# A seven-product block multiplication in three PSUM banks instead of four, with a new order of work

## The chip, the cores and the metric

The kernel runs on one core of one Trainium2 chip. The core has a matrix engine (TensorE, PE in the profile, with its weight loads as PEld), a vector engine (VectorE, DVE), a scalar engine (ScalarE, ACT), GpSimd (POOL) and a sync engine (SP). POOL, SP and ACT issue DMAs here. The metric is the device time of one execution in microseconds (us); of several runs the median is given.

## The reference

Eight batches of eight heads with 576 positions of 64 elements go through a retention layer (attention scores times a decay, no softmax), the result is laid out as 4608 tokens of 512 features, and a two-layer network with an exact gelu follows:

```python
scores = scale * np.matmul(q, k.transpose(0, 1, 3, 2))
ret = scores * Dmat            # Dmat = gamma[h] ** (i - j) for i >= j, else 0
x = np.matmul(ret, v)          # then (8, 576, 8, 64) -> (4608, 512)
h = x @ w_in                   # 512 -> 2048
g = 0.5 * h * (1.0 + erf(h * inv_sqrt2))
out = g @ w_out                # 2048 -> 512
```

The output is float32; the kernel multiplies in bfloat16 and adds up in float32.

## The kernel before

**Tokens and blocks.** The tokens are cut into 36 units of 128 (a batch's 576 positions are four chunks of 128 and a tail of 64; two tails share a unit) and nine blocks of 512 tokens, t = 0 to 8, four units each. Retention runs by units in groups: scores (tile `sc`), a mask on DVE (`ret`), products with the scaled values (`o_ps`), a running state (`u_ps`, copied to `u_sb`), and a multiplication on DVE that writes the block's input `xT`. Before it each unit's q and k are turned, the first ten units on TensorE (`qk_ps`, L235), the others by DMA from SP, and v is scaled by `dv` (`vh`, L819 to L830), by DVE in one operation or by ACT in eight, as the list `VH_ACT` (L174) says.

**First product.** Block by block, x times w_in. Blocks 0 and 1 do it plainly (`hT`). From block 2 on the hidden units are taken in four sets (0 to 3); a set is either plain ("p3") or a *unit* of seven products of half the size in place of eight (Strassen's scheme in Winograd's form), whose sums need three banks of PSUM: Y, Z and X. `LAYOUTS` (L192) says which sets are units and which run interleaved ("01" is two units in turn), `PRODUCTS` (L201) the order of the seven. ACT applies gelu and writes `g`.

**Second product.** Blocks 1 to 8 multiply g by w_out by the same scheme, in the order `SECOND` (L202). One piece is four matmuls of 256 columns; a product has two row tiles and two parts, so 16 matmuls. Products 1 and 2 have a bank for each row tile (A). Bank B takes 6; DVE adds product 1 onto it (`on`, L1241 to L1244); 5 is then added by TensorE. Bank C takes 7, and later 4. Bank D takes 3. What leaves them, in before:

- ACT copies 2 out as part of c11, 7 as the start of c22 (`p7`), B after 6 as the start of c21 (`u2`), B after 5 as the start of c12 (`u4`). These copies are `out_of` (L1246).
- DVE adds C onto c21, B onto c22 and D onto c12. These are `out_plus` (L1250), which also gives the bank back.
- Product 5 waits for `u2`, product 4 for `p7` (`BEHIND2`).

c11, c12, c21 and c22 are the quarters of the block's output tile `o_sb`, two halves of 256 rows by two of 256 columns; SP stores each half when its quarters are done. The last block does this for each row tile by itself and stores quarters, from SP (c21) or ACT (the rest).

**Order of the work.** Nothing is ordered at run time: while the program is built, a planner keeps a clock for each engine, an estimated duration, a due time and the operations it waits for, and writes out each engine's instructions in the order in which it places them. For ACT, DVE and SP it takes, among operations that can start within a slack of the earliest (`SLACK` before 20 us), the one due first (L87 and L1593). TensorE takes one of three kinds: single operations of retention; a *macro*, a stretch of small-tile matmuls of one group's retention step, once its due time (the group's need plus `SHIFT`) is reached, at least `GAP_A` or `GAP_B` after the last stretch; or a piece of the first or second product, out of the next `LOOK` pieces of the current run (a run is one block's first or second product), the one that can start first. Groups in `APART` have their scores in a macro of their own, `BEFORE` ahead of the need; the others' scores are in the macro of the group before. `LEAD`, `SPREAD`, `EASE` and `HOLD` set needs, the earliest start of a scaled v and how macros hold back other work. Until 16 us the planner fills gaps on TensorE with matmuls on zeros (`warm`). Loads are issued by POOL in the fixed list `ORDER`.

Of the kernel before, what the change touches and what calls it, by code (L numbers as in the profile page):

```python
# [107 lines left out]
def kernel(  # L108
# [9 lines left out]
    nc = tc.nc  # L118
    ctx.enter_context(tc.manual_schedule())

    B, H, S, D = q.shape
# [5 lines left out]
    C = 128  # L127
# [37 lines left out]
    n = v_order.index(pair_of[1, 1][0])  # L165
# [5 lines left out]
    N_VH = 5  # L171
    N_RET = 3
    N_Q = 4
    VH_ACT = [5, 6, 7, 8, 9, 10, 21, 22, 23, 24, 26, 27, 28, 29, 30, 31, 33, 34, 35]  # L174
    HOT = 10.1
    N_WARM = 8
    SLACK = 0.2
    CUTS = (0, 128, 256, 384, 512)
    AHEAD = 6
    WIDE = [2, 10, 14, 12, 4]  # L180
# [2 lines left out]
    FAST = 1  # L183
    FETCH = 4.0
    BUSY_FETCH = 6.2
    GAP_A = 4.7
    GAP_B = 0
    SHIFT = {4: -0.5, 5: 4.0, 6: 4.5, 7: -2.0, 8: 6.0, 9: 0.5, 10: 0.5, 11: -6.0, 12: -3.5, 13: -0.5, 14: -3.5, 15: -0.5, 16: -4.5, 17: -2.0, 18: -3.5, 19: 0.0, 20: 1.0}
    APART = [3, 5, 6, 7]
    BEFORE = 8.1  # L190
    UNIT_FROM = 2
    LOOK = 12  # L192
    HOLD = 6
    LAYOUTS = {2: ['01', '2', 'p3'], 3: ['01', '2', 'p3'], 4: ['1', '02', 'p3'], 5: ['0', '1', '2', 'p3'], 6: ['01', '23'], 7: ['01', '23'], 8: ['0', '12', 'p3']}
    LEAD = 8.9
    SPREAD = 5.6
    EASE = 9
    ORDER = ("k2 k1 pos q1 wi0 q3 k3 q2 v1 v2 v3 wi4 wi7 wi1 wi5 v4 k4 q5 wi6 k5 wi3 wi2 q4 wo0 v5 wo4 wo1 q9 wo5 "
             "q8 v7 wo6 v6 q7 q6 wo2 k7 v10 wo7 wo3 k6 q10 k8 v8 k10 k9 v9").split()
    K_ORDER = [0, 1, 8, 9, 2, 3, 10, 11, 4, 5, 12, 13, 6, 7, 14, 15]  # L200
    PRODUCTS = "3251467"  # L201
    SECOND = "1267534"  # L202
    LAYOUT = {t: ["p0", "p1", "p2", "p3"] for t in range(2, N_BLK)}
    for t in range(UNIT_FROM, N_BLK):
        LAYOUT[t] = LAYOUTS[t]
# [14 lines left out]
    P = Plan()  # L220
    P.later = {}
    T = P.T
    add = P.add
# [36 lines left out]
    def release(b, when):  # L260
        held.remove(b)
        free_at[b] = when
# [280 lines left out]
    for item in ORDER:  # L543
        what = item.rstrip("0123456789")
# [433 lines left out]
    LEFT = {"2": 0, "1": 1, "5": 2, "6": 3, "7": 4}  # L978
    RIGHT = {"3": 0, "1": 1, "4": 2, "6": 3, "7": 4}
    BEHIND = {"5": "m3", "4": "q", "6": "dif", "7": "c21"}  # L980
    BANK2 = {"1": "A", "2": "A", "6": "B", "5": "B", "7": "C", "4": "C", "3": "D"}
    BEHIND2 = {"2": "p1", "5": "u2", "4": "p7"}
    OPENS = "1673"

    def g_of(t, m):
        kp = m % 8 // 2
# [259 lines left out]
    def out_of(key, n, what):  # L1246

        nc.scalar.copy(target(key, what), chain[key][n][1])  # L1248

    def out_plus(key, n, what):  # L1250
        to = target(key, what)
        nc.vector.tensor_tensor(to, to, chain[key][n][1], op=ALU.add)  # L1252
        release(chain[key][n][0], T["dve"] + 0.12)

    def add_second(key, width, pe, due):
        nm = f"c{key}"
        half = 0.5 if width == 1 else 1.0
        act, dve = 0.07 + 0.43 * half, 0.07 + 0.53 * half  # L1260
        def room(h, t=key[1]):
            return lambda: 0.0 if ("o", t, h) in fold else o_ring[h].at()
        for n, r in enumerate(key[2]):
            add(nm + f"p1{r}", "act", 0.285, [pe["1"][n]] + ([nm + f"p1{key[2][0]}"] if n else []), lambda r=r: first_of(key, width, r),
                due["1"] + 0.1, at=None if n else m_ring.at)
            add(nm + f"c11{r}", "act", 0.285, [pe["2"][n]], lambda r=r: c11_of(key, r), due["2"] + 0.3, at=room(0))
        add(nm + "on", "dve", dve, pe["6"] + [nm + f"p1{r}" for r in key[2]], lambda: onto(key), due["6"] + 0.1)
        add(nm + "p7", "act", act, pe["7"], lambda: out_of(key, "C", "c22"), due["7"] + 0.1, at=room(1))
        add(nm + "u2", "act", act, [nm + "on"], lambda: out_of(key, "B", "c21"), due["6"] + 0.5, at=room(1))
        add(nm + "u4", "act", act, pe["5"], lambda: out_of(key, "B", "c12"), due["5"] + 0.1, at=room(0))  # L1270
        add(nm + "c21", "dve", dve, pe["4"] + [nm + "u2"], lambda: out_plus(key, "C", "c21"), due["4"] + 0.1)
        add(nm + "c22", "dve", dve, pe["5"] + [nm + "p7", nm + "u4"], lambda: out_plus(key, "B", "c22"), due["5"] + 0.6)
        add(nm + "c12", "dve", dve, pe["3"] + [nm + "u4"], lambda: out_plus(key, "D", "c12"), due["3"] + 0.1)

    def add_chain(key, width, pe, due):

# [44 lines left out]
    for run in stream:  # L1321
        for one in run:
# [7 lines left out]
            elif one[0] == "u":  # L1330
                _, t, kp, p = one
                key = f"c{('u', t, kp)}"
                deps = [f"x{i}" for i in range(4 * t, 4 * t + 4)]
                deps += [f"ui{kp}.{LEFT[p]}"] if p in LEFT else []
                deps += [f"xs{t}.{RIGHT[p]}"] if p in RIGHT else []
                deps += [key + BEHIND[p]] if p in BEHIND else []
                add(nm, "pe", piece_time(one), deps, lambda one=one: unit(one), W[one], DRAIN, banks=int(p in "321"))
                if p == PRODUCTS[-1]:
                    add_chain(("u", t, kp), 2, {q_: [f"mlp{('u', t, kp, q_)}"] for q_ in PRODUCTS},
                              {q_: W["u", t, kp, q_] for q_ in PRODUCTS})  # L1340
            elif isinstance(one[2], str):
                _, t, p, r, n, part = one
                kps = (2 * part, 2 * part + 1)
                rs = next(x for x in rows_at_once(t) if r in x)
                key = f"c{('2', t, rs)}"
                deps = []
                if p in G_SUM:
                    deps += [f"gs{t},{part}.{G_SUM[p]}"]
                else:
                    deps += gelus_of(t, kps, int(p != "1"))  # L1350
                deps += [f"ws{kp}.{W_SUM[p]}" for kp in kps] if p in W_SUM else []
                deps += [f"land wo{kp + 4 * (p != '1')}" for kp in kps] if p in "123" else []
                deps += [key + BEHIND2[p] + (str(r) if p == "2" else "")] if p in BEHIND2 else []
                add(nm, "pe", piece_time(one), deps, lambda one=one: fast(one), W[one], DRAIN,
                    banks=int(not part and (p == "1" or p in OPENS and r == rs[0])))
                if p == SECOND[-1] and r == rs[-1] and part:
                    at_ = {q_: {x: W["2", t, q_, x, SECOND.index(q_), 1] for x in rs} for q_ in SECOND}
                    add_second(("2", t, rs), len(rs), {q_: [f"mlp{('2', t, q_, x, SECOND.index(q_), 1)}" for x in rs] for q_ in SECOND},
                               {q_: max(at_[q_].values()) for q_ in SECOND})
                    if t < N_BLK - 1:  # L1360
                        add(f"st{t},1", "sp", 1.1, [key + "c21", key + "c22"], lambda t=t: store(t, 1), W[one])
                        add(f"st{t},0", "sp", 1.1, [key + "c12"] + [key + f"c11{x}" for x in rs], lambda t=t: store(t, 0), W[one] + 1)
                    else:
                        for h, c, on in ((0, 0, f"c11{r}"), (1, 1, "c22"), (0, 1, "c12"), (1, 0, "c21")):
                            add(f"st{t},{h}{c}.{r}", *(("act", 0.6) if on != "c21" else ("sp", 0.6)), [key + on],
                                lambda t=t, r=r, h=h, c=c, e=nc.scalar if on != "c21" else nc.sync:
                                store(t, h, slice(256 * c, 256 * c + 256), (r,), False, e), W[one] + 4.0 + c)
            else:
                _, t, ts, n0, n1 = one
                ms = K_ORDER[n0:n1]  # L1370
                gl = [o for o in W if o[0] == "1" and o[1] == t and any(o[2] <= m < o[2] + o[3] for m in ms)
                      and o[4] < ts * 128 + 128 and o[5] > ts * 128]
                before = [f"mlp{('2', t, ts, 2 * n0 - n1, n0)}"] if n0 else []
                add(nm, "pe", piece_time(one), [f"land wo{m // 2}" for m in ms] + [f"gelu{o}" for o in gl] + before,
                    lambda one=one: plain(one), W[one], DRAIN, banks=int(n0 == 0))
                if n1 == N_DF:
                    add(f"po{t},{ts}", "act", 0.5, [nm], lambda t=t, ts=ts: plain_out(t, ts), W[one] + 0.5,
                        at=lambda t=t, ts=ts: 0.0 if ("o", t, ts // 2) in fold else o_ring[ts // 2].at())
                    if ts % 2:
                        add(f"st{t},{ts // 2}", "sp", 1.1, [f"po{t},{ts - 1}", f"po{t},{ts}"], lambda t=t, ts=ts: store(t, ts // 2), W[one] + 1)  # L1380
# [155 lines left out]
    def begun(one):  # L1536
# [7 lines left out]
            return one[2] in "12" or (one[2] in OPENS and one[3] == rs[0]) or BANK2[one[2]] in chain.get(("2", one[1], rs), ())  # L1544
        return True

    def pe_candidates():
        got = []
        for op in P.open["pe"]:
# [9 lines left out]
        for run in heads:  # L1559
# [8 lines left out]
                if not op.waits and not (hold and op.banks) and begun(one):  # L1568
                    got.append((max(T["pe"], op.ready, nth_free(op.banks)), 2, W[one], op))
            window += 1  # L1570
            if window >= (AHEAD if run[0][1] < 2 else 1):
                break
        got = [g for g in got if g[0] < NEVER / 2]
        if macros and not any(g[1] == 0 for g in got):
# [88 lines left out]
```

## Time and profile before

| what | us |
|---|---|
| median of 3 runs | 280.59 (280.51 to 280.66) |
| the profiled execution | 281.12 |
| its span, first to last instruction | 279.2 |
| PE's share in the chain that ended last | 79% |
| DMA's share in it | 14% |
| first matmul; first product without gaps from | 1.19; 17.82 |
| last matmul group ends; last DVE add ends | 275.97; 276.43 |
| DVE adds of L1252: 21 of 128x512, 6 of 128x256 | 14.1, 2.5 |
| ACT copies of L1248: 21 of 128x512, 6 of 128x256 | 12.1, 2.2 |
| ACT scaled v, L829: 152 operations for 19 units | 41.3 |
| DVE scaled v, L826: 17 units | 11.6 |
| store from SP, 256 KB, issue to landing | 3.4 |

Rows of the profile name an engine, a line of the kernel, an operation and its tiles, out<-in. A group has its busy time and the mean of one operation, then the idle time of the engine just before it and what ended that. In a timeline the first two numbers are start and length in us, xN merges N operations in a row, and the bracket holds the idle time and its releaser. Ends of matmuls are modelled, so their starts tell more. In the table of stretches each engine has its busy time and number of operations; then come the clock granted to TensorE (1.00 is full speed), the busy share of the DMA engines, and GB/s.

### The profile page before, as it was taken

What the parts mean: (1) busy time and instruction counts of PE and PEld (TensorE: products, weight loads), DVE (VectorE), ACT (ScalarE), POOL (GpSimd) and SP (SyncE); (2) the same over time, 40 slices, a digit from 0 to 9 for tenths busy, and PEclk for the clock granted to TensorE, in tenths of its full rate; (3) what the DMA queues carried; (4) which work ended last, traced back from release to release, by engine and by line L of the source; (5) the groups of instructions that cost most, each with busy time, mean ns of one, the idle gap of its engine ahead of it and who ended that gap; (6) DMA issues with size and microseconds to landing.
All of it is one profiled execution on the core that took longest, in us unless ns stands there. A gap on an engine that the chain in (4) does not pass through costs nothing.

```text
span 279.2 us, 8727 instructions
## 1 busy us (share of the span) xinstructions
PE 273.0 (98%) x3626; PEld 216.2 (77%) x3626; DVE 228.7 (82%) x437; ACT 181.7 (65%) x446; POOL 110.4 (40%) x139
## 2 busy tenths in 40 slices
PE   7999999999999999999999999999999999999995
PEld 2675567478888688868886888778888888888684
DVE  5862554589989997999898999997899979969843
ACT  7766638786418823693559657975896689627840
POOL 8977688809755097311452725705000000000000
PEclk9999999999999999999999999999999999999999
DMA  9999999999999999999999999999600040003013
GB/s 150 161 187 179 190 175 173 178 169 165 149 142 177 193 134 151 134 236 99 142 197 88 128 160 222 116 113 121 190 2 2 6 151 2 2 22 131 0 40 113
DMA packets 152374, 35.55 MB, mean 127 GB/s; under 512 B 141072, under 2 KB 148240, under 8 KB 152336
## 3 DMA queue, kind: packets, MB, share of 16 engines
q0 software_dynamic: 115792, 17.97, 97.6%
q1 hardware_dynamic: 34544, 15.93, 31.0%
q10 hardware_dynamic: 2000, 1.11, 1.4%
q8 instruction: 28, 0.46, 0.7%
q14 instruction: 10, 0.08, 0.1%
HBM read 36.70 MB, written 9.44 MB: 165 GB/s over the span
## 4 chain that ended last, share of the span: by engine, by line
PE 79%; DMA 14%; POOL 5%; issue 1%; ACT 0%; DVE 0%; POOLq 0%
PE oT L231 37%; PE zT L231 11%; PE hT L231 9%; DMA w_out<-in_moe_w_out_dram 9%; PE yT L231 7%; PE o_ps L231 4%; DMA w_in<-in_moe_w_in_dram 3%; PE sc L231 2%; POOL qk_ld L522 2%; DMA qk_ld<-in_k_dram 2%; PE u_ps L231 2%; POOL w_in L528 1%; POOL v_ld L522 1%; PE xT__1851 L231 0%; PE xT__5150 L231 0%
## 5 line engine op out<-in xcount | busy, mean ns | idle before, releaser
L231 PEld LDWEIGHTS <-g 128*128 128x128 bf16 x576 | 55.2, 98 | 12.5 <-issue 0.4
L231 PEld LDWEIGHTS <-w_in 128*128 128x128 bf16 x528 | 47.2, 98 | 15.9
L231 PEld LDWEIGHTS <-wi_sum 128*128 128x128 bf16 x460 | 44.6, 98 | 7.1 <-issue 0.4
L231 PE MATMUL hT<-xT,w_in 128*128 128x256 bf16 (+2 forms) x344 | 49.0, 295 | 0.0
L231 PE MATMUL oT<-w_out,g 128*128 128x256 bf16 (+1 forms) x320 | 45.6, 294 | 0.1
L522 POOL DMA_DIRECT2D qk_ld<-in_q_dram x31 | 27.8, 898 | 38.9 <-DMA qkT<-qk_ld 24.2
L829 ACT ACTIVATE vh<-v_ld,dv 128x64 bf16<-128x64 bf16 x152 | 41.3, 348 | 1.0 <-DVE ret L657 1.0
L231 PEld LDWEIGHTS <-s 128*128 128x128 bf16 x384 | 36.8, 98 | 5.3 <-issue 0.4
L1104 ACT ACTIVATE g<-hT 128x512 bf16<-128x512 f32 (+1 forms) x58 | 31.5, 558 | 11.1 <-PE hT L231 10.4
L522 POOL DMA_DIRECT2D v_ld<-in_v_dram x31 | 28.0, 906 | 14.0 <-issue 6.7
L231 PE MATMUL oT<-w_sum,s 128*128 128x256 bf16 x256 | 32.6, 273 | 0.3 <-issue 0.3
L231 PE MATMUL oT<-w_sum,g 128*128 128x256 bf16 x256 | 31.1, 273 | 0.0
L1248 ACT COPY o_sb<-oT 128x512 f32<-128x512 f32 (+1 forms) x27 | 14.3, 539 | 23.7 <-PE oT L231 12.1
L522 POOL DMA_DIRECT2D qk_ld<-in_k_dram x31 | 28.0, 905 | 2.8 <-DMA v_ld<-in_v_dram 1.4
L1217 ACT ACTIVATE g<-zT 128x512 bf16<-128x512 f32 x46 | 26.4, 608 | 0.7 <-DVE zT L1226 0.6
L657 DVE TENSOR_TENSOR ret<-sc,msk 128x512 bf16<-128x512 f32 x36 | 22.9, 683 | 4.3 <-PE sc L231 4.3
L1252 DVE TENSOR_TENSOR o_sb<-o_sb,oT 128x512 f32<-128x512 f32 (+1 forms) x27 | 16.6, 626 | 10.5 <-PE oT L231 5.7
L834 ACT CAST u_sb<-u_ps 128x512 bf16<-128x512 f32 x19 | 11.3, 596 | 14.4 <-PE u_ps L231 12.5
L860 DVE TENSOR_TENSOR xT<-o_ps,dqT 128x512 bf16<-128x512 f32 x26 | 17.1, 683 | 1.9 <-PE o_ps L231 1.9
L573 DVE COPY qkT<-qk_ps 128x512 bf16<-128x512 bf16 x16 | 6.4, 421 | 13.9 <-PE qk_ps L235 13.8
L1226 DVE TENSOR_TENSOR zT<-q,zT 128x512 f32<-128x512 f32 x23 | 15.8, 692 | 2.1 <-PE zT L231 1.8
L575 ACT COPY q<-yT 128x512 f32<-128x512 f32 x16 | 9.0, 600 | 11.7 <-PE yT L231 11.7
(173 smaller groups left out, 470.6 us busy)
## 6 DMA issues: line engine op xcount, KB each, us to landing
out_dram<-o_sb SPq DMA_DIRECT2D x29, 256.0 KB, 3.4
qk_ld<-in_k_dram POOLq DMA_DIRECT2D x31, 128.0 KB, 7.2
qk_ld<-in_q_dram POOLq DMA_DIRECT2D x31, 128.0 KB, 7.5
v_ld<-in_v_dram POOLq DMA_DIRECT2D x31, 128.0 KB, 7.8
w_in<-in_moe_w_in_dram POOLq DMA_DIRECT2D x8, 256.0 KB, 8.1
w_out<-in_moe_w_out_dram POOLq DMA_DIRECT2D x8, 256.0 KB, 8.4
out_dram<-o_sb SPq DMA_DIRECT2D x7, 128.0 KB, 2.4
out_dram<-o_sb ACTq DMA_DIRECT2D x5, 128.0 KB, 1.9
```

Of the source, the lines that this page charges most:

```text
L231: return nc.tensor.matmul(*args, **more)
L522: nc.gpsimd.dma_start(dst, src[2 * bp + j, :, ci * C:ci * C + C, :].rearrange("h s d -> s h d"))
L575: nc.scalar.copy(dst, src)
L657: nc.vector.tensor_tensor(r, t, by, op=ALU.mult)
L829: nc.scalar.activation(vh[:, h], loaded[i][1][:, h], AF.Copy, scale=dv[:, h, ci:ci + 1])
L834: ins = (nc.vector.tensor_copy if engine == "dve" else nc.scalar.copy)(u_sb[t if bp >= FINE else ci % 2], u_bank[1])
L860: nc.vector.tensor_tensor(dst, o, dqT[:, :, ci * C:ci * C + C], op=ALU.mult)
L1104: nc.scalar.activation(g_of(t, m0)[:, m0 % 2:m0 % 2 + n, m0 // 8, lo:hi], hT, AF.Gelu)
L1217: nc.scalar.activation(target(key, what), chain[key][n][1], AF.Gelu)
L1226: nc.vector.tensor_tensor(to, chain[key]["q"], z, op=ALU.add)
L1248: nc.scalar.copy(target(key, what), chain[key][n][1])
L1252: nc.vector.tensor_tensor(to, to, chain[key][n][1], op=ALU.add)
```

## The change

Product 3 moves from bank D to bank B and to the end of the order. It is added by TensorE onto what is there (1 + 6 + 5), after DVE has added B onto c22 (`BEHIND2`: "3" waits for `c22`). One ACT copy of the finished sum is c12. The copy `u4` and the DVE add of c12 go, and so does bank D; B is given back after the copy of c12. In the last block the quarter c12 is stored from SP.

At the end of a run (`EDGE`) TensorE may look into the next one while one piece is left that needs no new bank. The parameters of the planner, the list `VH_ACT` (37 is no unit), the layouts of blocks 4, 5 and 7 and the order of the first product (6 ahead of 4) have new values.

```diff
-    VH_ACT = [5, 6, 7, 8, 9, 10, 21, 22, 23, 24, 26, 27, 28, 29, 30, 31, 33, 34, 35]
+    VH_ACT = [5, 6, 8, 9, 10, 11, 12, 13, 14, 15, 21, 22, 26, 27, 28, 31, 32, 33, 34, 37]
-    SLACK = 0.2
+    SLACK = 0.05
+    EDGE = 1
-    GAP_A = 4.7
-    GAP_B = 0
-    SHIFT = {4: -0.5, 5: 4.0, 6: 4.5, 7: -2.0, 8: 6.0, 9: 0.5, 10: 0.5, 11: -6.0, 12: -3.5, 13: -0.5, 14: -3.5, 15: -0.5, 16: -4.5, 17: -2.0, 18: -3.5, 19: 0.0, 20: 1.0}
-    APART = [3, 5, 6, 7]
-    BEFORE = 8.1
+    GAP_A = 3.5
+    GAP_B = 1.7
+    SHIFT = {4: -5.0, 5: 5.5, 6: 3.0, 7: -2.5, 8: 5.0, 9: -3.5, 10: -0.5, 11: -2.0, 12: -4.5, 13: -1.0, 14: -4.0, 15: -2.0, 16: -3.0, 17: 0.5, 18: -6.0, 19: -2.5, 20: 1.5}
+    APART = [3, 5, 6, 7, 8]
+    BEFORE = 3.8
-    LOOK = 12
-    HOLD = 6
-    LAYOUTS = {2: ['01', '2', 'p3'], 3: ['01', '2', 'p3'], 4: ['1', '02', 'p3'], 5: ['0', '1', '2', 'p3'], 6: ['01', '23'], 7: ['01', '23'], 8: ['0', '12', 'p3']}
-    LEAD = 8.9
-    SPREAD = 5.6
-    EASE = 9
+    LOOK = 18
+    HOLD = 3.9
+    LAYOUTS = {2: ['01', '2', 'p3'], 3: ['01', '2', 'p3'], 4: ['2', '30', 'p1'], 5: ['0', '12', 'p3'], 6: ['01', '23'], 7: ['10', '23'], 8: ['0', '12', 'p3']}
+    LEAD = 8
+    SPREAD = 6.5
+    EASE = 7.6
-    PRODUCTS = "3251467"
-    SECOND = "1267534"
+    PRODUCTS = "3251647"
+    SECOND = "1267543"
...
-    BANK2 = {"1": "A", "2": "A", "6": "B", "5": "B", "7": "C", "4": "C", "3": "D"}
-    BEHIND2 = {"2": "p1", "5": "u2", "4": "p7"}
-    OPENS = "1673"
+    BANK2 = {"1": "A", "2": "A", "6": "B", "5": "B", "3": "B", "7": "C", "4": "C"}
+    BEHIND2 = {"2": "p1", "5": "u2", "3": "c22", "4": "p7"}
+    OPENS = "167"
...
     def out_of(key, n, what):
 
         nc.scalar.copy(target(key, what), chain[key][n][1])
+        if what == "c12":
+            release(chain[key][n][0], T["act"] + 0.14)
 
     def out_plus(key, n, what):
         to = target(key, what)
         nc.vector.tensor_tensor(to, to, chain[key][n][1], op=ALU.add)
-        release(chain[key][n][0], T["dve"] + 0.12)
+        if what == "c21":
+            release(chain[key][n][0], T["dve"] + 0.12)
...
-        add(nm + "u4", "act", act, pe["5"], lambda: out_of(key, "B", "c12"), due["5"] + 0.1, at=room(0))
         add(nm + "c21", "dve", dve, pe["4"] + [nm + "u2"], lambda: out_plus(key, "C", "c21"), due["4"] + 0.1)
-        add(nm + "c22", "dve", dve, pe["5"] + [nm + "p7", nm + "u4"], lambda: out_plus(key, "B", "c22"), due["5"] + 0.6)
-        add(nm + "c12", "dve", dve, pe["3"] + [nm + "u4"], lambda: out_plus(key, "D", "c12"), due["3"] + 0.1)
+        add(nm + "c22", "dve", dve, pe["5"] + [nm + "p7"], lambda: out_plus(key, "B", "c22"), due["5"] + 0.1)
+        add(nm + "c12", "act", act, pe["3"], lambda: out_of(key, "B", "c12"), due["3"] + 0.1, at=room(0))
...
-                            add(f"st{t},{h}{c}.{r}", *(("act", 0.6) if on != "c21" else ("sp", 0.6)), [key + on],
+                            add(f"st{t},{h}{c}.{r}", *(("act", 0.6) if on in ("c22", f"c11{r}") else ("sp", 0.6)), [key + on],
...
+    def ending(run):
+
+        return run[0][1] > 1 and len(run) <= EDGE and not any(P.ops[f"mlp{one}"].banks for one in run) and run is heads_left()[0]
...
-            if window >= (AHEAD if run[0][1] < 2 else 1):
+            if window >= (AHEAD if run[0][1] < 2 else 1) and not ending(run):
                 break
```

## The prediction, made before the run

> **What bounds the kernel now.** I read the busy times of the page first, then the busy time by stretch, then the waits of TensorE, then the timeline around the second product and at the end.
>
> The busy times:
>
> ```profile
> PE 273.0 (98%) x3626; PEld 216.2 (77%) x3626; DVE 228.7 (82%) x437; ACT 181.7 (65%) x446; POOL 110.4 (40%) x139
> ```
>
> By stretch (start:end, length, then busy time of PE, PEld, DVE, ACT, POOL):
>
> ```profile
> 0.00:17.80 17.80, 16.07 (x166) 8.78 (x166) 13.38 (x47) 12.55 (x29) 16.55 (x25) 1.00 1.67 164
> 17.80:59.80 42.00, 41.19 (x489) 26.28 (x484) 20.73 (x45) 28.64 (x80) 29.01 (x37) 1.00 2.01 175
> 59.80:276.00 216.20, 215.70 (x2980) 181.10 (x2977) 194.15 (x346) 140.55 (x339) 64.89 (x78) 1.00 1.16 115
> ```
>
> What TensorE waited for, in all:
>
> ```profile
> PE warm L231 <- DVE ln_scale L352: 1.2, 1, 1.2
> PE qk_ps L235 <- DMA qk_ld<-in_k_dram: 0.7, 1, 0.7
> PE oT L231 <- issue: 0.3, 1, 0.3
> PE zT L231 <- ACT g L1217: 0.2, 1, 0.2
> ```
>
> TensorE is the bound: from 17.8 us to 276.0 it is idle for 0.81 + 0.50 = 1.31 us, at a granted clock of 1.00. Busy rows have modelled ends, so I also read the starts: sixteen 256-column matmuls take 1.74 us (189.90 to 191.64 below), 0.109 each, and a 512-column one 0.216. What a start is later than that is lost. Four losses stand out: 0.30 near 32.7 (twelve 512-column matmuls from 32.05, next row at 35.03, less a tile change of 0.09), 0.84 before 53.92 (eight from 51.35 should end at 53.08), 0.43 before 108.98 (one 256-column matmul at 108.44) and 0.37 before 171.85 (four from 171.04). Together 1.94 us: that, and the start, is all a new order can win. DVE, nearly always busy from 60 to 130 us, is not what TensorE waits for.
>
> **The matmuls.** Products, layouts and units keep their number: 28 pieces of four matmuls for each of eight blocks, and in blocks 4 and 5 three seven-product units and one plain block as before. 0.
>
> **Evacuation of the second product.** Per block one ACT copy (u4) goes and one (c12) comes; one DVE add into o_sb goes. Of the 27 adds of line 1252 (21 of 685 ns, 6 of 422) a third: 7 x 0.685 + 2 x 0.422 = 5.6 us of DVE's 228.7. TensorE hides this, since no wait of it names these adds: 0, and the bank that D no longer takes is also worth 0, because the piece behind the last product starts without a gap (195.13 + 1.75 = 196.88).
>
> **The new wait.** Product 3 goes onto the bank that c22 reads, so it waits for 5, then DVE's add. Behind it on TensorE stand the rest of 3 and everything later. Block 6 as it runs now, 7 at 189.90, 5 at 191.64, 3 at 193.39, 4 at 195.13:
>
> ```profile
> 189.90 1.91 PE L231 MATMUL oT<-w_sum,g 128*128 128x256 bf16 x16
> 190.17 0.70 DVE L1243 TENSOR_TENSOR oT<-oT,q 128x512 f32<-128x512 f32 x1 [0.20 <-PE oT L231]
> ...
> 190.90 0.59 ACT L1248 COPY o_sb<-oT 128x512 f32<-128x512 f32 x1 [0.63 <-DVE oT L1243]
> ...
> 191.64 1.91 PE L231 MATMUL oT<-w_sum,s 128*128 128x256 bf16 x16
> ...
> 193.39 1.91 PE L231 MATMUL oT<-w_out,s 128*128 128x256 bf16 x16
> 193.59 0.59 ACT L1248 COPY o_sb<-oT 128x512 f32<-128x512 f32 x1 [1.16 <-PE oT L231]
> ...
> 194.21 0.69 DVE L1252 TENSOR_TENSOR o_sb<-o_sb,oT 128x512 f32<-128x512 f32 x1 [0.48 <-ACT o_sb L1248]
> ...
> 195.13 1.91 PE L231 MATMUL oT<-w_sum,g 128*128 128x256 bf16 x16
> ```
>
> Another engine sees product 5 at 193.59, 0.20 after the next product starts. The add then ends at 193.59 + 0.69 = 194.28, and TensorE follows about 0.05 later (below, ACT ends at 171.80, PE starts at 171.85). Product 4, now between, lasts until 195.13: 0.80 us to spare, 0.19 with one other DVE operation in front (they follow at 0.61), 0.42 short with two. The wait that already exists is tighter: 5 waits for DVE's 0.70 and ACT's 0.59 behind 6, ready at 190.90 + 0.59 + 0.05 = 191.54 for a start at 191.64, and TensorE's waits show none for it. So 0; at worst 7 x 0.42 = +2.9; no gain. The Trainium skill (PSUM — Partial Sum Buffer, Summary: rules for kernel authors) speaks against the edit: while a bank is read, matmuls should go to a different one. Before does so for 3, which starts at 193.39 while ACT reads the other bank at 193.59; by that rule the wait would show, and the time would be the third rival's; by the rows it does not.
>
> **The end.** The last product is followed by an ACT copy instead of a DVE add:
>
> ```profile
> 274.06 1.91 PE L231 MATMUL oT<-w_sum,g 128*128 128x256 bf16 x16
> ...
> 275.58 1.21 SPq L1305 DMA_DIRECT2D out_dram<-o_sb  x2
> 276.01 0.42 DVE L1252 TENSOR_TENSOR o_sb<-o_sb,oT 128x256 f32<-128x256 f32 x1 [0.45 <-PE oT L231]
> ```
>
> The same copy of that size took 0.37 (272.52 in this view), so -0.05. The store stays on SP's queue, whose two earlier issues of 0.6 us end before it; c12's two stores leave ACT's queue. ACT then issues four stores late in the block (c22, three pieces, and one of c21), 4 x 0.6 = 2.4 us from about 272.1, done before the last copy at 276.0. If one of them stood in front of it, +0.6. In blocks 1 to 7 output half 0 is now stored last instead of half 1; its tile is written next by the following block's c11 (266.45 after an end at 251), against 3.4 us from issue to landing: 0.
>
> **Scores of group 8 apart.** One more stretch of small tiles among full ones:
>
> ```profile
> 75.94 1.47 PE L231 MATMUL oT<-w_sum,s 128*128 128x256 bf16 x12
> 77.34 0.64 PE L231 MATMUL sc<-qkT 64*64 64x128 bf16 x32
> 77.91 0.61 PE L231 MATMUL oT<-w_sum,s 128*128 128x256 bf16 x4
> ```
>
> Twelve matmuls from 75.94 are through at 77.25, the scores start at 77.34: 0.09. The scores take 0.57 to the next full matmul, against 0.48 inside a mixed stretch (56.14 to 56.62): 0.09 more. +0.2 (0 to +0.25).
>
> **Scaled v.** Units 7, 23, 24, 29, 30 and 35 go from ACT to DVE, and 11 to 15 and 32 the other way: 6 x 0.68 us of DVE and 6 x 2.2 of ACT (41.3 us over 19 units) each change places, 0 in sum; DVE wins 3.4 us where it is fullest. Block 4 now has set 3 as a unit, so the five sums of its weights (0.416 us each, w_in's line 1049) come before block 4 (139.8) instead of block 6 (196.9): 2.1 us of DVE earlier, where no wait of TensorE on DVE stands: 0.
>
> **The wait at 171.85.**
>
> ```profile
> 171.21 0.59 ACT L1217 ACTIVATE g<-zT 128x512 bf16<-128x512 f32 x1
> ...
> 171.85 0.60 PE L231 MATMUL zT<-xs,wi_sum 128*128 128x256 bf16 x4 [0.21 <-ACT g L1217]
> ```
>
> ACT was late since it waited 0.55 us for a DVE copy, and DVE ran without a pause. With 6 ahead of 4 in the first product's order, and units 23 and 24 off ACT, I take the whole: -0.38 (-0.38 to 0). That order can also cost: 7 waits for a gelu of 0.60 behind 4, and with 6 already done only the partner's 4 (0.44) covers it; with 0.10 for the two hand-overs it is 0.26 short at the last pair of a block where the 18 pieces looked at hold nothing else. Two blocks are all units, two pairs each: +1.0 at most; I take 0, because the order is made by readiness and 6 waits for two DVE operations.
>
> **Early waits.** The groups' due times move by up to 4.5 us (group 4: -0.5 to -5.0). The wait of 0.84 before 53.92 is a transpose on TensorE placed ahead of its load, though full matmuls (hT from 59.77) follow. The queue of loads keeps its order, so it lands when it did; only another place helps. -0.60 of 0.84, nearer to the whole as much other work is ready; bounds -0.84 to +0.84, one more of its kind. The losses of 0.43 and 0.30 have no releaser in the trace: 0 (-0.73 to +0.73).
>
> **Start and run ends.** SLACK changes which operation DVE and ACT take before 20 us: one DVE operation in front of a mask or out of it, ±0.61, taken as 0. EDGE lets TensorE look into the next run at a run's last piece; no wait stands there: 0.
>
> **Sum.** -0.05 + 0.20 - 0.38 - 0.60 = -0.83. The profiled execution took 281.12 (span 279.2, 1.9 around it), 0.5 over the median of 280.59, so the difference goes onto the median: 279.8.
>
> **Rivals.** *Nothing comes of it* (0.20): the relief of DVE is off TensorE's path, the waits stay or move, and -0.05 + 0.20 is left: 280.7. For it: no wait names the second product. *More at the start* (0.12): matmuls on zeros fill about 3.9 us between 7.15 and 16.2; a third less of them is -1.3 more: 278.5. *The new wait shows* (0.07): slower, on product 3, from two DVE operations in front of c22 on; DVE is full in blocks 1 to 5, so 5 x 0.42 + 0.15: 282.8. Against it: the 0.80 us. *A second early load wait* (0.13): one more 0.84 and the 0.15: 281.6. For it: groups due up to 4.5 us earlier behind an unchanged queue of loads.
>
> **How the numbers follow.** My forecast has 0.48, with its own range 279.2 to 280.3. A measurement tells about 0.2%, 0.56 us, from no change, so faster means below 280.0: two thirds of the forecast (0.32) and the gain at the start (0.12), 0.44. Within: the rest of the forecast (0.16) and the empty rival but for 0.03, 0.33. Slower: 0.07 + 0.13 + 0.03 = 0.23. The range runs from 279.0, the forecast's side of the gain at the start, to 281.7, over the second load wait; outside lie 282.8 and 278.5, 0.19.
>
> **What would show it.** Right: no wait of TensorE on ACT's g, none or less on in_k_dram, 18 adds in line 1252's place and 27 copies, the last instruction an ACT copy of 0.37, a TensorE gap under 0.05 between 4 and 3. Wrong: a wait of oT on DVE's o_sb there, idle time of TensorE over 1.3 us after 17.8, or useful matmuls in a row from a time far from 17.8.

## The result, and the profile after

The changed kernel is slower. Beside runs of the kernel before on the same chip it took 281.96 us against 280.73 (6 runs each, ratio 1.004, 95% interval 1.0026 to 1.0053), and in a second comparison 281.55 against 280.93 (12 and 19 runs, 1.0024, 1.001 to 1.0037): 0.6 to 1.2 us. The profiled execution took 281.36, span 279.4.

The busy times of the changed kernel:

```profile
PE 273.0 (98%) x3624; PEld 215.8 (77%) x3624; DVE 227.9 (82%) x436; ACT 176.9 (63%) x438; POOL 110.4 (40%) x139
```

By stretch, with the columns as before:

```profile
0.00:17.80 17.80, 15.16 (x155) 7.78 (x156) 13.49 (x47) 12.02 (x28) 16.44 (x25) 1.00 1.66 163
17.80:59.80 42.00, 42.00 (x500) 27.09 (x498) 21.51 (x47) 27.74 (x74) 29.07 (x37) 1.00 1.99 176
59.80:276.00 216.20, 215.68 (x2975) 180.98 (x2973) 192.89 (x344) 136.80 (x337) 64.86 (x78) 1.00 1.08 115
```

The waits of TensorE:

```profile
PE warm L232 <- DVE ln_scale L353: 1.2, 1, 1.2
PE qk_ps L236 <- DMA qk_ld<-in_q_dram: 0.6, 2, 0.3
PE zT L232 <- ACT g L1218: 0.4, 2, 0.2
PE sc L232 <- DVE qkT L574: 0.2, 1, 0.2
```

TensorE does the same work and from 17.8 us on is idle for 0.00 + 0.52 = 0.52 us by these rows, less than the 1.31 of before, and yet the kernel is slower: busy time with modelled ends hides the loss, and only the starts show it. 11 matmuls fewer are started by 17.8 us (9 of them useful ones), the first product runs without gaps from 18.33 instead of 17.82, and the wait on ACT's g now stands twice. The second product of block 6, which answers to the timeline shown of before (product 7 at 189.91, 5 at 191.67, 4 at 193.41, 3 at 195.16):

```profile
191.67 1.91 PE L232 MATMUL oT<-w_sum,s 128*128 128x256 bf16 x16
...
193.41 1.91 PE L232 MATMUL oT<-w_sum,g 128*128 128x256 bf16 x16
193.67 0.69 DVE L1255 TENSOR_TENSOR o_sb<-o_sb,oT 128x512 f32<-128x512 f32 x1 [0.17 <-issue]
...
195.16 1.91 PE L232 MATMUL oT<-w_out,s 128*128 128x256 bf16 x16
```

DVE's add of c22 ends at 194.36 and product 3 starts at 195.16, where 4 ends: the new wait has 0.80 us to spare. The end:

```profile
276.25 0.37 ACT L1249 COPY o_sb<-oT 128x256 f32<-128x256 f32 x1 [0.50 <-PE oT L232]
```

The ends of matmuls are modelled, so I counted lost time from their starts in all traces: the distance from one start to the next less the columns at full rate (0.109 us for 256 columns; small tiles that run at the same time share it), with matmuls on zeros counted as lost. The wait at 53 is part of the column to 54.6, "no releaser" part of the column 107 to 110:

| trace | to 54.6 us | wait for a load near 53 | 54.6 to 107 | 107 to 110 | of it no releaser | 110 to 270 |
|---|---|---|---|---|---|---|
| before | 14.47 | 0.84 | 2.01 | 0.72 | 0.43 | 3.76 |
| before, again | 14.09 | 0.49 | 2.02 | 0.99 | 0.71 | 3.76 |
| after | 14.07 | 0.13 | 2.06 | 0.47 | 0.18 | 4.59 |
| after, again | 14.23 | 0.15 | 2.16 | 0.28 | 0 | 4.51 |

Two columns hardly differ between two executions of one program, and there after loses up to 0.1 and 0.8 us more. The others differ between executions of one program: before lost 0.84 in one for a load near 53 and 0.49 in the other. The profiled executions of before (281.12 and 281.21) lie above its medians of 280.73 and 280.93, those of after (281.36 and 281.34) below its own of 281.96 and 281.55, so the traces' difference of 0.2 is smaller than the medians' of 0.6 to 1.2.

### The profile page after: what moved, and what is told of

Same layout as the page of the kernel before. It is cut to its first block, busy times and chain, and to the rows that moved or that the text cites. A ratio compares the mean times of both kernels' runs of the same rounds, so it can differ in the third digit from the quotient of the medians.

```text
span 279.4 us, 8712 instructions
## 1 busy us (share of the span) xinstructions
PE 273.0 (98%) x3624; PEld 215.8 (77%) x3624; DVE 227.9 (82%) x436; ACT 176.9 (63%) x438; POOL 110.4 (40%) x139
## 4 chain that ended last, share of the span: by engine, by line
PE 88%; ACT 4%; DMA 2%; POOL 2%; DVE 1%; issue 1%; POOLq 0%; ACTq 0%
PE oT L232 41%; PE hT L232 16%; PE zT L232 9%; PE yT L232 5%; PE o_ps L232 5%; PE sc L232 3%; ACT g L1218 3%; DMA qk_ld<-in_q_dram 2%; PE u_ps L232 2%; POOL qk_ld L523 2%; PE qk_ps L236 1%; DVE q L1197 1%; DVE t L574 1%; PE warm L232 1%; ACT o_sb L1249 1%
## 5 line engine op out<-in xcount | busy, mean ns | idle before, releaser
L232 PE MATMUL hT<-xT,w_in 128*128 128x256 bf16 (+2 forms) x344 | 49.6, 295 | 0.0
L830 ACT ACTIVATE vh<-v_ld,dv 128x64 bf16<-128x64 bf16 x152 | 42.1, 347 | 0.3 <-DVE ret L658 0.3
L1197 DVE TENSOR_TENSOR q<-q,zT 128x512 f32<-128x512 f32 x23 | 15.1, 681 | 5.0 <-ACT q L576 4.5
L1255 DVE TENSOR_TENSOR o_sb<-o_sb,oT 128x512 f32<-128x512 f32 (+1 forms) x18 | 11.2, 627 | 5.7 <-PE oT L232 5.2
```

The source lines that it names most:

```text
L232: return nc.tensor.matmul(*args, **more)
L830: nc.scalar.activation(vh[:, h], loaded[i][1][:, h], AF.Copy, scale=dv[:, h, ci:ci + 1])
L1197: nc.vector.tensor_tensor(q_, q_, chain[key]["Z"][1], op=ALU.subtract)
```

## The experiments

Each was timed beside the kernel before on the same chip, which had medians of 280.93, 281.15, 280.98 and 280.93 us in the four sets. Unless said otherwise the edit is on the changed kernel.

**The changed kernel again** (no edit).

> The changed kernel once more, for a second profile beside a median. Its first profiled execution (281.36 us) was the fastest of six (median 281.96), so up to 0.6 us of the loss isn't in that trace. Theory 'start' (DVE takes an operation of dqT in front of masks, first product later by 0.43): the time is again 282.0 and the lost time of TensorE at 12 us is 10.0 in both traces. Theory 'thin margins' (early work placed closer to its loads, so executions differ): waits of TensorE on DMA or ACT in this trace that the first one lacks, about 0.3 to 0.6 us in all before 60 us.

281.55 us, ratio 1.0024. Lost time at 12 us is 10.45, so the start is as late as in the first trace or later, but at 54.6 us it is 14.23, no more than before. No waits were added before 60 us: the first trace lacks nothing there.

**The start: SLACK as before.**

```diff
-    SLACK = 0.05
+    SLACK = 0.2
```

> The changed kernel with SLACK 0.2 as before. Theory 'start': the loss at 12 us goes back from 10.0 to 9.5 and the time falls by about 0.4, to 281.6. Theory 'new wait' or 'thin margins': the start may change but the time stays at 282.0 within 0.2.

281.97 us, ratio 1.0047 (1.0029 to 1.0065). The start came back (9.57 lost at 12 us, 12.73 at 20 us against 13.10), and 0.69 us was lost near 53 instead of 0.13: 14.34 in all at 54.6. The theory "start" fell. The rows show where such a gain goes. The timeline of the kernel with the layouts of before (last in this section), TensorE's line on `qk_ps` near 53:

```profile
54.01 0.61 PE L236 MATMUL qk_ps<-ident,qk_ld 128*128 128x128 bf16 x8 [0.82 <-DMA qk_ld<-in_k_dram]
```

and the same in the first trace of after:

```profile
53.44 0.61 PE L236 MATMUL qk_ps<-ident,qk_ld 128*128 128x128 bf16 x8
```

One waits 0.82 for its load, the other shows no wait there, and they start 0.57 apart. In the fifteen traces this turn starts between 53.3 and 54.2 us, however much was done before it.

**The three banks alone**, on the kernel before: `SECOND`, `BANK2`, `BEHIND2`, `OPENS`, `out_of`, `out_plus`, `add_second` and the last stores as in the change, all parameters of the order as before.

```diff
-    SECOND = "1267534"
+    SECOND = "1267543"
...
-    BEHIND2 = {"2": "p1", "5": "u2", "4": "p7"}
+    BEHIND2 = {"2": "p1", "5": "u2", "3": "c22", "4": "p7"}
```

> The kernel before with the three banks alone (product 3 last, onto B, one copy of c12), all parameters of the order as before. Theory 'new wait' (product 3 waits for DVE's add of c22): slower by 0.4 to 2.9, gaps on TensorE between products 4 and 3. Theory 'start' or 'thin margins' (the parameters do it): within 0.2 of before, or faster by 0.05 from the end.

281.99 us, ratio 1.0048 (1.0029 to 1.0067): slower by 1.1, but not for the reason expected. No gap stands between 4 and 3. The gaps are between 7 and 5: 0.37 at 75.4, 0.64 at 105.1, 0.20 at 162.8, 0.29 at 246.0. The timeline of this kernel at the second of them:

```profile
104.44 0.69 DVE L1243 TENSOR_TENSOR oT<-oT,q 128x512 f32<-128x512 f32 x1
...
105.16 1.07 ACT L1248 COPY o_sb<-oT 128x512 f32<-128x512 f32 x2 [2.29 <-DVE oT L1243]
...
105.80 0.92 PE L231 MATMUL oT<-w_sum,s 128*128 128x256 bf16 x7 [0.47 <-ACT o_sb L1248]
```

and of the kernel before at the same place:

```profile
104.46 0.69 DVE L1243 TENSOR_TENSOR oT<-oT,q 128x512 f32<-128x512 f32 x1
...
105.18 1.07 ACT L1248 COPY o_sb<-oT 128x512 f32<-128x512 f32 x2 [2.29 <-DVE oT L1243]
105.18 1.04 PE L231 MATMUL oT<-w_out,s 128*128 128x256 bf16 x8
...
106.06 1.04 PE L231 MATMUL oT<-w_sum,s 128*128 128x256 bf16 x8
```

DVE's add is late in both (104.44 and 104.46: behind two `xT` operations), ACT's copy u2 starts at 105.16 and 105.18 and 5 can't start before. Before has product 3 (oT<-w_out,s) here: it opens a bank of its own, waits for nothing, and two of its pieces go ahead of 5. The order of the pieces in the trace shows the same in the blocks at 154.0, 210.7 and 238.2, with one piece each. In three banks 3 comes last by force, and no piece of it can stand there. This accounts for three of the four gaps (105.1, 162.8, 246.0); in the fourth of these blocks 5 follows 7 at 219.64 without one. The gap at 75.4 stands in a block where before has no piece of 3 ahead of 5: there 7 starts 0.43 earlier than in before's first trace (73.72 against 74.15), DVE's add only 0.13 (74.45 against 74.58), so 5 has to wait for ACT's copy.

**The parameters alone**: the changed kernel with the four banks of before.

```diff
-    SECOND = "1267543"
+    SECOND = "1267534"
...
-    BEHIND2 = {"2": "p1", "5": "u2", "3": "c22", "4": "p7"}
+    BEHIND2 = {"2": "p1", "5": "u2", "4": "p7"}
```

> The changed kernel with the four banks of before, all parameters of the order as after. Theory 'start' and 'thin margins': as slow as after, 281.8 to 282.2, since the parameters do it. Theory 'new wait': back at 280.7.

282.9 us, ratio 1.0074 (1.0057 to 1.009), slower than expected by any theory. All four combinations were timed on this chip:

| us | parameters of before | parameters of after |
|---|---|---|
| four banks | 280.93 | 282.90 |
| three banks | 281.99 | 281.55 |

The two halves of the change don't add up. The three banks cost 1.1 with the parameters of before and win 1.35 with those of after; the parameters cost 2.0 with four banks and win 0.4 with three, and that 0.4 isn't sure, since the first comparison had the whole change 1.2 above before. The trace of the parameters alone lost 0.65 without a releaser at 108.4 (told at the end), 0.32 near 53, 0.33 ahead of product 5 at 134.4 and 0.31 at 237.7; after's first trace has 0.18, 0.13 and no such loss at the last two. Why this order suits four banks so badly stays open.

**The kernel before again** (no edit).

> The kernel before once more, for a second trace. Its first profiled execution (281.12) was above its median (280.6 to 280.9) and held a wait of 0.84 us for a load of k at 53.9. Theory 'one execution' (that wait is mostly chance, so the changed kernel's shorter one is no gain): the wait is below 0.5 here, TensorE's lost time at 60 us is 14.0 to 14.4 instead of 14.72, and from 60 to 270 us it is again 6.3. Theory 'the gain is real and something else is lost': 0.8 again at 53.9.

281.21 us, ratio 0.9996 (0.9975 to 1.0016). The wait near 53 is 0.49 here, with 14.39 lost at 60 us: "one execution" holds. The wait of 0.37 on ACT's g stands in both traces, at 171.3.

**The first product's order.**

```diff
-    PRODUCTS = "3251647"
+    PRODUCTS = "3251467"
```

> The changed kernel with the first product's order as before (4 ahead of 6). Theory 'product 7 too early' (7 of a unit that runs alone is placed right when its gelu should end, and waits 0.38 at 142.9 and at 171.8): both waits shrink to under 0.1 each and the time falls by 0.4 to 0.8. Theory 'layouts' (the lone unit in front of a pair has the wait whatever the order): both stay, same time within 0.3.

281.97 us, ratio 1.0032 (1.0015 to 1.005). Both waits of 0.37 stay (143.3 and 172.1): the order of the list doesn't matter.

**The gelu of c21 seen later.** The planner's lag after that operation:

```diff
-            add(nm + w, "act", acts["act"] + 0.0, pe[p], lambda w=w: quadrant(key, w), due[p] + 0.3, at=room[w])
+            add(nm + w, "act", acts["act"] + 0.0, pe[p], lambda w=w: quadrant(key, w), due[p] + 0.3, at=room[w],
+                lag=0.6 if w == "c21" and key[0] == "u" else 0.12)
```

> The changed kernel, but the planner takes a unit's c21 gelu as seen by TensorE 0.6 us after its end instead of 0.12, so that it puts other pieces in front of product 7. Theory 'product 7 too early': both waits of 0.38 go, the time falls by 0.5 to 0.8 to about 281.0, no worse than before. Theory 'it comes back elsewhere': the waits go, and the gap shows at other rows; same time within 0.3.

283.9 us, ratio 1.0098 (1.0075 to 1.0121). The two waits went, and 7.0 us were lost from 110 to 270 instead of 4.5 (among them 0.40 at 134.3, 0.38 at 154.3, 0.52 at 174.6, 0.42 at 196.8). Neither theory had it this bad.

**Group 8's scores with the others.**

```diff
-    APART = [3, 5, 6, 7, 8]
+    APART = [3, 5, 6, 7]
```

> The changed kernel without group 8 in APART. Theory 'stretch': one stretch of small tiles less (27 instead of 28), faster by 0.2. Theory 'elsewhere': no change within 0.2, since the scores then make another stretch longer or later.

281.66 us, ratio 1.0013 (0.9997 to 1.003). From 54.6 to 270 us this trace enters small tiles 23 times, as after's second trace and as before. The stretch that was costed at 0.2 isn't there, and the time can't be told from after's 281.55.

**Product 3 only after 5, on the kernel before.** Four banks, the same copies and adds; one dependence more:

```diff
+                deps += [f"mlp{('2', t, '5', x, SECOND.index('5'), 1)}" for x in rs] if p == "3" else []
```

> The kernel before, four banks, with one thing taken away: product 3 may start only when 5 is done, so that it can't be put ahead of 5 as in four of the eight blocks (96.5, 154.0, 210.7, 238.2). Theory 'lost filler' (in three banks nothing can be done while 5 waits for ACT's copy u2; the kernel with the banks alone waits 0.38, 0.64, 0.20 and 0.29 there): waits of oT on ACT's o_sb of 0.2 to 0.6 in these blocks, slower than before by 0.6 to 1.2. Theory 'ACT and DVE order' (those waits come from the moved copies and adds): no such waits, within 0.3 of before.

281.78 us, ratio 1.0031 (1.0016 to 1.0045): slower by 0.8, as "lost filler" said. TensorE's waits in this kernel, and the block where before puts a piece of 3 at 219.17:

```profile
PE oT L231 <- ACT o_sb L1248: 0.8, 2, 0.5
```

```profile
218.81 1.08 ACT L1248 COPY o_sb<-oT 128x512 f32<-128x512 f32 x2
...
219.45 1.80 PE L231 MATMUL oT<-w_sum,s 128*128 128x256 bf16 x15 [0.32 <-ACT o_sb L1248]
```

Gaps of 0.63, 0.25, 0.48 and 0.29 us stand ahead of 5 in just the four blocks in which before has 3 there. The wait on ACT's g at 171 is only 0.06 here, since the plan behind each gap is another one. So with the parameters of before this order alone, without any change of bank, copy or add, costs about what the three banks cost: 0.5 to 1.3 us by its interval, against 0.8 to 1.9 for the banks.

**The copy t made known to the planner.** A unit's gelu of c12 on ACT reads the bank that t is copied from, and in the trace it waits for that copy. The changed kernel:

```profile
141.02 0.69 DVE L574 COPY t<-yT 128x512 f32<-128x512 f32 x1
...
141.80 0.60 ACT L1218 ACTIVATE g<-yT 128x512 bf16<-128x512 f32 x1 [0.52 <-DVE t L574]
...
142.94 0.60 PE L232 MATMUL zT<-xs,wi_sum 128*128 128x256 bf16 x4 [0.21 <-ACT g L1218]
```

ACT takes the gelu of c21 at 142.30, right behind it. The planner lists only the product for c12's gelu, so it has both gelus, and product 7 behind them, too early whenever DVE makes the copy.

```diff
-            add(nm + w, "act", acts["act"] + 0.0, pe[p], lambda
+            add(nm + w, "act", acts["act"] + 0.0, pe[p] + ([nm + "raw"] if w == "c12" and key[0] == "u" else []), lambda
```

> The changed kernel, where the planner knows that a unit's c12 gelu on ACT follows the copy t of the same bank (as the trace has it: ACT waits 0.52 for DVE's copy at 141.8 and 170.7). Theory 'unplanned wait' (product 7 is placed too early because the planner starts that gelu, and c21's behind it, 0.5 too soon): the two waits of 0.38 go, faster by up to 0.7, 281.0. Theory 'it comes back elsewhere' (as with the later c21): they go, and other waits of the same sum come.

281.98 us, ratio 1.0031 (1.0016 to 1.0046). Both waits are gone, which fits the cause, and the sum is not: 0.20 at 104.8, 0.31 at 133.7, 0.17 at 208.2 and 0.31 at 236.8 came. 4.76 us are lost from 110 to 270.

**The same edit on the kernel before.**

> The kernel before, four banks, where the planner knows that a unit's c12 gelu on ACT follows the copy t of the same bank. The prediction took -0.38 for the wait at 171.85. Theory 'recoverable' : that wait goes and nothing else comes, faster by 0.3 to 0.4, 280.6, the fastest so far. Theory 'it comes back elsewhere' (as in the changed kernel with the same edit): the wait goes, others of 0.3 to 1.0 in all come, same or slower.

281.71 us, ratio 1.0029 (1.0011 to 1.0046). The wait on ACT's g is gone here too, and the kernel is slower by 0.8. Its profiled execution took 284.5 us, the slowest of twelve, and can't be used for a count; what happened in it is told at the end.

**Product 6 ahead of 2.**

```diff
-    SECOND = "1267543"
+    SECOND = "1627543"
```

> The changed kernel with the second product in the order 1 6 2 7 5 4 3, so that two products and not one lie between 6 and 5, which waits for u2. Theory 'lost filler': the waits behind u2 (0.18 at 75.3, 0.19 at 160.6, 0.14 at 161.1) go, faster by 0.3 to 0.5. Rival: 6 waits for DVE's sum of g earlier than now and TensorE waits there: same or slower.

286.93 us, ratio 1.0196 (1.0159 to 1.0234). The small waits ahead of 5 did go, but a gap of 3.07 us at 192.7 came that neither theory had, so the order itself isn't judged by this run. It isn't one bad execution: all six took 284.57 to 288.72. What the gap is, and what it did to the clock, is told at the end.

**The layouts of blocks 4 and 5 as before.**

```diff
-    LAYOUTS = {2: ['01', '2', 'p3'], 3: ['01', '2', 'p3'], 4: ['2', '30', 'p1'], 5: ['0', '12', 'p3'], 6: ['01', '23'], 7: ['10', '23'], 8: ['0', '12', 'p3']}
+    LAYOUTS = {2: ['01', '2', 'p3'], 3: ['01', '2', 'p3'], 4: ['1', '02', 'p3'], 5: ['0', '1', '2', 'p3'], 6: ['01', '23'], 7: ['10', '23'], 8: ['0', '12', 'p3']}
```

> The changed kernel with the layouts of blocks 4 and 5 as before. Theory 'layouts' (the lone unit ahead of a pair, now in both blocks, gives the waits of 0.38): one of the two is left, as before, faster by 0.3 to 0.4. Theory 'unplanned wait': both stay or move with the order of DVE's copy, same time within 0.3.

281.78 us, ratio 1.0021 (1.0005 to 1.0037). Both waits stay (143.1 and 171.9): "layouts" fell.

No kernel tried here is faster than the one before.

## Why the prediction was wrong

The forecast was 279.8, 0.83 us under before; the kernel came out 0.6 to 1.2 over it. The forecast's gain was made of two waits, and neither was won: the terms -0.60 and -0.38 below. A third step, taken at 0, is the one that the experiments show to cost time.

**The step that failed** is the one that set the freed bank at 0 because the piece behind the last product starts without a gap, and the wait of 5 for u2 at 0 because the trace shows no wait there. Both rows were read rightly, in block 6. But in four other blocks of before product 3 stands ahead of 5 and covers that wait, on the bank that the change takes away. The prediction looked for what the moved product waits for (c22, harmless: 0.80 us to spare, as worked out) and not for what was covered by the product while it could move. With the parameters of before, three banks alone cost 1.1 us and product 3 tied behind 5 alone 0.8. Reading the order of the pieces in all eight blocks of before would have shown it. In the changed kernel itself little of this is left: its new order starts 5 late by 0.18 at 75.3 and by 0.19 at 160.6, where a first matmul behind small tiles is late by about 0.13 anyway. The largest single loss that it has and before lacks is the second wait on ACT's g, 0.38. Whether other costs come from the freed bank or from the new parameters isn't told apart there, since the two halves don't add up.

**The early wait (-0.60)** was mis-sized from one execution. It was 0.84 in that one and 0.49 in the next of the same program, and between 0.13 and 0.98 in executions of changed kernels. Nor was its loss free to win. In before TensorE starts earlier and then stands for the load; in after it starts 0.5 us later, which the prediction named as possible, and has next to no wait there. The two about cancel: to 54.6 us after lost 14.07 and 14.23, before 14.47 and 14.09, on average 0.13 less instead of 0.60.

**The wait at 171.85 (-0.38)** was not won but doubled: it stands at 171.80 in after, and a second of the same kind at 142.94, so the term came out at +0.38. Its cause was read rightly (ACT behind a DVE copy), the cure was not: relief of DVE doesn't help where the planner places 7 too early. Taken out by the planner it came back as other waits in both kernels.

**Scores apart (+0.20)** came out at about 0, since the number of small-tile stretches stayed 23 between 54.6 and 270 us. **The end (-0.05)** came as worked out: the copy takes 0.37 and the add took 0.42; from the last start of a matmul (275.94 and 275.70) to the end of the span it is 3.46 and 3.5. **The new wait (0)** came as worked out. The rule of the Trainium skill (PSUM — Partial Sum Buffer, Summary: rules for kernel authors), that matmuls go to a different bank while one is read, does not speak against the edit as the prediction had it: while DVE reads bank B (193.67 to 194.36) TensorE runs 4 on bank C, and 3 starts on B at 195.16, behind the read. What the fourth bank was worth was the freedom to go first.

The rival with a second early load wait stood at 281.6, near the measured time. That is luck: the traces of after have no such wait.

**The sum by what was found:** after loses up to 0.1 us more from 54.6 to 107 and 0.8 more from 110 to 270, about 0.9 in all; the medians differ by 0.6 and 1.2. Of the 0.8 the rows name 0.38 at 142.5 (product 7), 0.14 at 161.1 (ahead of product 7), and 0.2 on the first full matmul behind small tiles, the larger part of it at 160.6 and 235.5. What the new parameters do for the three banks is known as a difference of medians (281.99 against 281.55), not wait by wait.

## What to carry to other kernels

Before an operation is tied behind another, look where it stands in every repetition of the plan: if it is sometimes put ahead of a waiting one, its freedom is the cover, and the profile shows no wait just because of it. A wait seen in one execution is a gain only if a second execution of the same program has it too, above all one for a load. On an engine that is busy all the time, removing one planned wait reshuffles what follows, so judge such edits by the sum over a long stretch and not by the wait.

## What the runs showed that was not expected

**A wait that nothing releases, at a fixed count.** The gap near 108 us, put down to issue, stands in front of the 1371st or 1372nd matmul in seven of the kernels, with 0.18 to 0.75 us. In two executions of one program it was 0.43 and 0.71 (before) or 0.18 and 0 (after). A DMA transpose of SP runs at the time. It was far longer twice: in the profiled execution of the kernel before with the copy t known (before the 1362nd matmul there; that trace has 16 records fewer than before's),

```profile
107.55 5.49 SPq L613 DMA_TRANSPOSE qkT<-qk_ld  x2
...
107.80 0.28 PE L231 MATMUL oT<-w_sum,s 128*128 128x256 bf16 x1
109.67 1.61 PE L231 MATMUL oT<-w_sum,s 128*128 128x256 bf16 x7 [1.59 <-issue]
```

and with 6 ahead of 2, before the 2521st matmul, some nine times 128 later:

```profile
190.09 8.96 SPq L614 DMA_TRANSPOSE qkT<-qk_ld  x3
...
195.91 2.74 PE L232 MATMUL oT<-w_sum,s 128*128 128x256 bf16 x12 [2.90 <-issue]
```

A matmul here is two instructions (the profile of before counts 3626 weight loads and 3626 matmuls), so 128 of them are 256. The Trainium skill (Runtime: NRT & Kernel Launch, Instruction fetch mechanics) says that instructions are fetched by DMA in blocks of 256 and that crossing a block's end is mostly hidden. The counts fit that; the times here are not hidden. The DMA packets in the traces point to the fetch too. One queue in the profile is named for instructions (packets, MB, share of 16 engines' span):

```profile
q8 instruction: 28, 0.46, 0.7%
```

That is 28 packets of 16,384 bytes, one for some 129 of the 3624 matmuls of after. With 6 ahead of 2 the 19th packet ran from 193.48 to 194.65, when 2520 matmuls had started and TensorE stood still; in the other traces it had started by the 2439th at the latest. TensorE went on 1.26 us after it landed. The 10th belongs to the gap near 108: in the nine traces with that gap TensorE goes on 1.34 to 1.82 us after it lands, and in the second trace of after, which has no gap, the 1371st matmul starts 2.13 us after it. So these gaps are waits for instructions, as far as times can show it. What makes a packet late isn't shown: transposes ran at the time, but in the second trace of after, without a gap, they ran too, and that the fetch waits for them was not tried.

**The clock behind such a gap.** In the first of these two executions the columns of the stretches (granted clock third from the end) show:

```profile
109.70:113.20 3.50, 3.50 (x18) 2.43 (x18) 1.47 (x4) 0.59 (x1) 1.75 (x2) 0.51 2.71 148
113.20:120.00 6.80, 6.80 (x64) 6.10 (x63) 5.75 (x12) 3.92 (x8) 1.52 (x2) 1.00 1.90 124
```

After 1.87 us from one start to the next TensorE ran at half its clock (0.51) for 3.5 us, 0.213 us for each matmul of 256 columns instead of 0.109, so the gap of 1.76 cost 1.7 more. Behind the gap of 3.07 the clock was 0.56 from 196 to 199 us. The Trainium skill (TensorE: Matmul & The Clock Gate, Part 1) gives an idle window of about 3.4 us for the fall to half clock; here a gap of little more than half of that was enough, while gaps up to 0.98 us (the kernel with the layouts of before, near 53) left the clock at 1.00.
